# A new written-out order of work for one transformer block on one core

## The chip, the cores and the metric

The kernel runs on one core of a Trainium2 chip. The metric is the time of one execution in microseconds (us) as the device measures it; for a kernel the median of its runs is given.

## The reference

One transformer block without masks: 2048 rows of 640 numbers in bfloat16, linear attention with 32 heads of 20 features, then a gated feed-forward part with 1536 inner features. In short:

```python
x = A_x                                             # 1 x 2048 x 640
q, k, v = heads(layernorm(x) @ wqkv)                # 32 heads of 20
pq, pk  = q @ w_phi[h], k @ w_phi[h]                # per head, 20 x 20
phi_q = concat(softmax(pq), softmax(-pq))           # 40 features, phi_k likewise
kv, z = phi_k^T @ v, sum_s phi_k
o = (phi_q @ kv) / (phi_q . z + 1e-6)
h = x + o @ wo
g, u = layernorm(h) @ w_gate, layernorm(h) @ w_up
out = h + (g * u) @ w_down
```

## The kernel before, in words

The 2048 rows are 16 tiles of 128 rows (t = 0 to 15). The kernel first builds a graph of small operations, 1032 in all, each with a name, an engine, its buffers and the code that emits it. A table of text, `PLAN`, gives every operation a due time, an engine (where it may run on more than one) and the numbers of the slots that its buffers take. The function `arrange` sorts the operations by due time, and that order, engine by engine, is the program. The due times are used for nothing but the order; waits follow from the data and from who used a slot before. So a plan changes when something is issued and where it is kept, and never what is computed.

An entry reads `name:due:engine:slots`. An empty or missing engine means the operation's first choice, 1 means its second.

The names that matter here:

- `x0`, `x1`, `x3`, ... load tiles of x; `wk*`, `wv*`, `w5`, `wo*`, `wg*`, `wu*`, `wd*` load weights (line 283). Each may be issued from SP's queue (SyncE) or from that of ACT (ScalarE). `wqt*` loads a part of the Q weights transposed (line 307).
- `warm*`: matmuls on zeros that keep TensorE (PE) busy until data arrive (lines 363, 368).
- `L1s`, `L1a`, `L1l`, `L1e`, `L1n`, `xn`: mean, variance and normalisation of a tile (lines 424 to 449). `xt` transposes the normalised tile: on PE for tiles 0 and 1 (line 458), by a DMA transpose from SP's queue for the others (line 467).
- `id*`, `gl*`, `va1`, `ekz`: constants that POOL (GpSimd) writes. `gl0`, `gla`, `glb` make a block mask (lines 329 to 336).
- `Ph0`, `Ph1`, `Ph2` multiply that mask with w_phi (loaded as `w5`) into Phi (line 376). `WT` transposes the K weights on PE (line 388), `F1` and `F0` multiply Phi into the K and Q weights (line 407, the fold), `WTe`, `xte` and `Fe` copy PSUM to SBUF.
- `V`, `K`, `Q`: projections of a tile (line 478, ten matmuls of about 320 columns). `Kx`, `Ks`, `Kr`, `Ke`, `Kn` and `Qx`, `Qs`, `Qr`, `Qb`, `Qe`, `Qn`: the two softmaxes of the K and Q features over ACT, DVE (VectorE) and POOL; `Qx` is lines 547 and 549. `Ve` copies V.
- `KV`: sum of phi_k times v over all tiles (line 522). `KVe` masks it.
- `qT`: DMA transpose of phi_q from SP's queue (line 571). `N`: phi_q times KV (line 584). `dd`, `rl`, `rd`, `o` divide. `oT`: DMA transpose of o (line 615). `O`: times wo (line 621). `h` adds x. `hc`, `L2q`, `L2v`, `L2r`: second normalisation. `hT`: DMA transpose of h (line 649).
- `U<block>_<f>_<0 or 1>`: gate and up matmuls (line 664) of a block of rows; block 0 is tiles 0 and 1, block 1 tiles 2 to 5, block 2 tiles 6 to 9, block 3 tiles 10 to 13, block 4 tiles 14 and 15. `g` copies the gate, `u` multiplies (lines 669, 672). `D`: down projection of a tile (line 683), `y` scales and adds (line 695), `w` stores (line 697). Tile 15's `D` is cut into three parts.

PSUM has eight banks; V, K, Q, N, O and D take two each, a U one. Six slots hold phi_q (`ph`) and six its transpose (`phT`), so `Qx` of a tile waits until the `qT` of the tile that had the slot before has landed.

The order itself comes from these few lines:

```python
for o in sorted(G.ops, key=lambda o: (o.key, o.i)):
    o.start = o.key
    order[o.eng].append(o)
    o.alldeps = dict(o.deps)
    for b, k0 in zip(o.acq, o.slots):
        b.slots = list(range(k0, k0 + b.n))
        for k in b.slots:
            for u in last[b.pool, k].users if (b.pool, k) in last else G.init.get(b.pool, ()):
                o.alldeps.setdefault(u, u in G.init.get(b.pool, ()))
            last[b.pool, k] = b
```

Of the kernel before, what the change touches and what calls it, by code (L numbers as in the profile page):

```python
# [59 lines left out]
L1e2:12.968 L1n2:13.248 wqt2:11.56 L1n5:12.518:1 xn5:12.802::3 xt5:13.62 K1_0:12.049::6 K1_1:12.32 K1_2:12.591 K1_3:12.862 xn4:13.332::0 K1_4:13.133  # L60
Kx1_0:13.603::0 Kx1_1:14.187 V1_0:13.404::4 V1_1:13.675 K0_3:13.946 K0_4:14.217 V1_2:14.488 mk0:13.472 va1:13.532 Kx0_0:14.771::1 xt4:14.93 Kx0_1:15.355
L1s11:13.862 xn2:15.939:1:2 Ks1:14.923::0 Kr1:16.754 Ke1:17.045 L1s10:16.316 L1s7:17.103 L1a10:17.89 Kn1:17.379 wqt1:16.24 V1_3:14.759 V1_4:15.03 V0_2:15.301
V0_3:15.572 V0_4:15.843 phz:19.692 K3:16.114::6 Ve1:17.191::0 L1s6:17.999 Ve0:17.775::1 L1a11:18.786 Kx3_0:18.359::2 Kx3_1:18.943 L1a7:18.895 L1a6:19.004
L1l6:19.527 L1e6:19.853 x8:17.55 L1n6:20.408 V3:17.47::2 xt2:18.03 wqt3:19.34 K5:18.826::4 Kx5_0:20.382::3 Ks0:19.113::1 wqt4:20.65 L1n7:20.506:1 Kx5_1:20.966
V4:20.182::0 xn7:21.55:1:1 xn6:20.71::3 Kr0:22.365 L1l10:22.511 xt6:21.96 Ke0:22.693 Kn0:23.027 x12:23.27 L1e10:22.839 L1n10:25.34 Ve4:22.932::2 xt7:23.75
V5:21.538::6 Ve5:23.516::3 K2:22.894::4 V2:24.25::0 Kx2_0:24.45::4 Kx2_1:25.034 L1n11:25.564 Ks3:21.24::2 L1s8:22.633 Kr3:25.618 Ks5:23.42::3 Ve2:25.806::4
wu4:25.06 F0_4:25.606::6 Fe0_4:26.39 x14:25.54 KV0:25.925::4,5 wo0:26.02 L1a8:24.813 KV1:26.258 mk1:25.788 L1s9:24.922 L1a9:25.832 L1l8:26.974 Ve3:27.156::5
L1e8:27.74 Ks2:25.941::0 L1s13:27.334 L1a13:28.244 L1n8:28.353:1 V6:26.591::0 L1n9:28.02 Kr2:27.833 Ke2:28.124 F0_0:27.947::6 Fe0_0:28.464 Kr5:29.048 wu0:26.5
xn9:28.528::0 xt9:29.166 Kn2:28.458 xn11:29.058::2 xt11:30.476 xn8:29.588::3 xt8:31.786 Ve6:29.194::6 K4:28.266::2 L1s12:30.118 Kx4_0:29.822::1 Kx4_1:30.406
Ke3:30.99 K7:29.622::6 Ks4:31.142::1 Kx7_0:31.178::0 L1s15:32.535 L1s14:33.322 Kx7_1:31.762 xn10:34.109::1 xt10:34.747 F0_2:30.978::0 Fe0_2:32.346 Kn3:31.324  # L70
V7:31.297::2 Kr4:32.93 Ke4:33.221 rqz:33.637 wu1:36.057 Ve7:33.367::7 F0_3:32.653::6 Fe0_3:33.951 Kn4:33.674 KV2:32.972 L1a14:34.639 K6:33.305::0
# [16 lines left out]
KV11:71.629 KV12:71.962 KV13:72.295 Kn14:69.144 Ve14:71.829::7 KV14:72.628 KV15:72.961 mk2:71.457 KVe1:73.492 Q6:73.294::6 qT3:65.636::4 Qr4:72.413::0
Qb4:72.757 KVe0:73.742 N0:74.661::0 Qr13:72.951::2 dd0:75.192::0 Qe4:73.097 rd0:75.407 Qx6_0:74.859::2 qT2:69.214::5 N2:74.994::2 dd2:75.697::1 Qb13:73.295
rl2:75.913 rd2:76.267 Qn4:73.494 qT4:75.185::0 o0:75.821::0 Q7:75.327::4 oT0:76.689::0 Qx6_1:76.447 o2:76.592::1 oT2:77.999::1 Qe13:77.057 Qn13:77.364  # L90
qT13:79.309::5 N1:76.718::0 dd1:77.347::0 rd1:77.562 o1:77.976::2 Qx7_0:77.176::4 Qx7_1:77.786 N9:77.264::6 dd9:78.731::0 Q11:77.597::2 Qx11_0:79.162::5
# [833 lines left out]
```

## Time and profile before

| | us |
|---|---|
| median of 3 runs | 271.68 |
| range of the runs | 271.24 to 466.2 |
| the profiled execution | 271.81 |
| its span, first to last instruction | 270.1 |

| engine | busy us | share of the span |
|---|---|---|
| PE, matmuls | 264.2 | 98% |
| PE, weight loads (beside the matmuls) | 178.2 | 66% |
| DVE | 158.6 | 59% |
| ACT | 126.7 | 47% |
| POOL | 69.4 | 26% |

In the views of the profile, times are counted from the first instruction. In a group or a piece of the timeline, the first number is its start, the second its length, `x10` the number of instructions in it, and the square bracket the idle time of the engine ahead of it with what ended that. PEld is PE's weight load; SPq and ACTq are DMAs issued from the queues of SP and ACT. In the table by stretches, each engine has its busy time and instruction count, and PEclk is the granted clock of PE (1.00 is full). The chain is followed back from the instruction that ended last.

### The profile page before, as it was taken

To read this page: it belongs to the slowest core of one execution; us is meant where nothing else is said; L and a number is where in the kernel's file an instruction comes from. 1 tells how busy PE (TensorE), PEld (TensorE's weight loads), DVE (VectorE), ACT (ScalarE), POOL (GpSimd) and SP (SyncE) were. 2 spreads that over 40 slices of the span, in tenths; PEclk is the share of its full clock that TensorE was granted. 3 is DMA by queue.
4 is the path that set the end of the run, shared out by engine and by line. 5 is a ranking of instruction groups with operands and counts; after the bars stand their busy time and mean duration, and the time that the engine had idled before them with its cause. 6 is when DMAs were issued, how large, how long until landed. Compare 5 with 4: busy or idle time off the path is not lost.

```text
span 270.1 us, 5194 instructions
## 1 busy us (share of the span) xinstructions
PE 264.2 (98%) x2092; PEld 178.2 (66%) x2105; DVE 158.6 (59%) x299; ACT 126.7 (47%) x319; POOL 69.4 (26%) x81
## 2 busy tenths in 40 slices
PE   7999999999999999999999999999999999999996
PEld 5777777777777688756556667774554466544775
DVE  4999989887988968956855243232243131352422
ACT  3999999998677684534435021112232220122000
POOL 1365799999735301060000000000000000000000
PEclk9999999999999999999999999999999999999999
DMA  6999966699758998757820005330011000010003
GB/s 190 287 182 184 274 190 245 135 227 188 180 86 160 139 153 157 106 102 139 213 49 2 0 0 100 102 71 1 0 41 22 0 0 27 25 49 2 0 24 109
DMA packets 67944, 28.09 MB, mean 104 GB/s; under 512 B 59088, under 2 KB 66640, under 8 KB 67920
## 3 DMA queue, kind: packets, MB, share of 16 engines
q1 hardware_dynamic: 67776, 27.60, 49.0%
q8 instruction: 16, 0.26, 0.4%
q10 hardware_dynamic: 144, 0.16, 0.2%
q14 instruction: 8, 0.07, 0.1%
HBM read 11.00 MB, written 2.62 MB: 50 GB/s over the span
## 4 chain that ended last, share of the span: by engine, by line
PE 90%; DMA 4%; ACT 1%; DVE 1%; POOL 1%; issue 1%; DVEq 0%; POOLq 0%
PE ps L664 38%; PE ps L478 23%; PE ps L683 19%; PE ps L621 6%; DMA scratch<-ph 3%; PE ps L522 2%; PE ps L584 2%; PE ps L407 1%; DMA x_all<-in_A_x_dram 1%; ACT ph L547 1%; POOL Phi L376 0%; DVE st L424 0%; DVE st L425 0%; DVE Wp L695 0%; ACT gt L669 0%
## 5 line engine op out<-in xcount | busy, mean ns | idle before, releaser
L664 PE MATMUL ps<-xnT,Wgu 128*128 128x512 bf16 (+1 forms) x587 | 105.5, 335 | 0.7
L664 PEld LDWEIGHTS ps<-xnT,Wgu 128*128 128x128 bf16 x600 | 58.1, 98 | 43.4 <-DVE ev L672 0.2
L669 ACT ACTIVATE gt<-ps 128x512 bf16<-128x512 f32 (+1 forms) x60 | 29.5, 509 | 92.0 <-PE ps L664 67.9
L478 PE MATMUL ps<-Wp,xnT 128*128 128x320 bf16 (+1 forms) x480 | 68.4, 299 | 0.0
L672 DVE TENSOR_TENSOR ev<-ps,gt 128x512 bf16<-128x512 f32 (+1 forms) x60 | 33.2, 579 | 51.1 <-PE ps L664 37.0
L478 PEld LDWEIGHTS ps<-Wp,xnT 128*128 128x128 bf16 x480 | 45.5, 97 | 17.3
L683 PE MATMUL ps<-Wd,ev 128*128 128x320 bf16 (+2 forms) x396 | 53.3, 295 | 0.0
L683 PEld LDWEIGHTS ps<-Wd,ev 128*128 128x128 bf16 x396 | 38.1, 98 | 15.0 <-DVE ev L672 0.3
L514 POOL TENSOR_TENSOR ek<-ek,SR 128x1280 bf16<-128x1280 bf16 x16 | 37.6, 2361 | 5.5 <-ACT SR L499 3.2
L695 DVE SCALAR_TENSOR_TENSOR Wp<-ps,rs,x_all 128x640 bf16<-128x640 f32 (+3 forms) x18 | 14.6, 809 | 38.1 <-PE ps L683 38.0
L494 DVE TENSOR_REDUCE SR<-ek 128x64 f32<-128x1280 bf16 x16 | 23.5, 1471 | 5.1 <-ACT ek L490 4.8
L642 POOL TENSOR_SCALAR ln<-mv 128x1 f32<-128x1 f32 x4 | 0.8, 191 | 98.3 <-ACT ek L638 98.2
L552 DVE TENSOR_REDUCE S<-ph 128x66 f32<-128x1320 bf16 x16 | 24.1, 1520 | 0.2
L621 PE MATMUL ps<-Wo,Wp 128*128 128x320 bf16 x160 | 23.8, 299 | 0.0
L547 ACT ACTIVATE ph<-ps 128x600 bf16<-128x600 f32 x32 | 21.2, 677 | 4.2 <-PE ps L478 2.2
L566 POOL TENSOR_TENSOR ph<-ph,RQ 128x660 bf16<-128x660 bf16 x16 | 20.8, 1308 | 4.6 <-ACT RQ L562 4.4
L490 ACT ACTIVATE ek<-ps 128x640 bf16<-128x640 f32 x32 | 21.0, 705 | 1.9 <-PE ps L478 1.8
L621 PEld LDWEIGHTS ps<-Wo,Wp 128*128 128x128 bf16 x160 | 15.5, 98 | 6.1
L638 ACT ACTIVATE ek<-x_all,mv 128x640 bf16<-128x640 bf16 x16 | 13.1, 821 | 10.4 <-DVE x_all L627 10.3
L627 DVE SCALAR_TENSOR_TENSOR x_all<-ps,x_all 128x640 bf16<-128x640 f32 x16 | 13.1, 821 | 6.6 <-PE ps L621 6.5
L611 DVE TENSOR_TENSOR o<-ps,sm 128x660 bf16<-128x660 f32 x16 | 13.2, 836 | 0.8 <-ACT sm L604 0.6
L559 POOL TENSOR_TENSOR RQ<-RQ 128x32 f32<-128x32 f32 x15 | 3.5, 241 | 28.9 <-ACT RQ L555 28.9
(70 smaller groups left out, 169.9 us busy)
## 6 DMA issues: line engine op xcount, KB each, us to landing
out_dram<-Wp SPq DMA_DIRECT2D x15, 160.0 KB, 1.8
x_all<-in_A_x_dram SPq DMA_DIRECT2D x6, 320.0 KB, 4.5
Wgu<-in_B_w_up_dram SPq DMA_DIRECT2D x5, 384.0 KB, 6.1
Wd<-in_B_w_down_dram SPq DMA_DIRECT2D x4, 480.0 KB, 5.2
Wgu<-in_B_w_gate_dram SPq DMA_DIRECT2D x5, 384.0 KB, 4.3
ev<-in_A_wqkv_dram SPq DMA_DIRECT2D x5, 160.0 KB, 3.8
Wp<-in_A_wqkv_dram SPq DMA_DIRECT2D x5, 160.0 KB, 4.9
x_all<-in_A_x_dram SPq DMA_DIRECT2D x3, 160.0 KB, 3.1
```

The costliest lines, as they stand in the source:

```text
L478: ins = e.matmul(pb(b, hb)[:, 0:n1 - n0], lhsT=T["xnT"][:, NC - 1 - c, P * t:P * (t + 1)], rhs=T["Wp"][:, POS[kind], c, n0:n1], start=(c = ...
L490: G.op("act", "%sx%d_%d" % (nm, t, s), lambda e, s=s, b=b, ek=ek: e.activation(out=T["ek"][:, ek.slots[0], 0:2 * D].rearrange("p (b h s f) ...
L494: G.op("dve", "%ss%d" % (nm, t), lambda e, ek=ek, sr=sr: e.tensor_reduce(out=T["SR"][:, sr.slots[0], 0, :], in_=T["ek"][:, ek.slots[0], 0: ...
L514: G.op("pool", "Kn%d" % t, lambda e, eng, ek=ek, sr=sr: e.tensor_tensor(out=T["ek"][:, ek.slots[0], 0:2 * D].rearrange("p (h f) -> p h f", ...
L547: e.activation(out=v[:, 0:10].rearrange("p (b g) j f -> p b g j f", b=2), in_=pp(b, 0, 300).rearrange("p b (g j f) -> p b g j f", j=3, f=D ...
L552: G.op("dve", "Qs%d" % t, lambda e, t=t, ph=ph: e.tensor_reduce(out=T["S"][:, t, 0:66].rearrange("p (g k) -> p g k", k=6), in_=pv(ph).rear ...
L566: return e.tensor_tensor(out=v, in0=v, in1=T["RQ"][:, rq.slots[0], 1, 0:33].rearrange("p (g j) -> p g j", j=3).unsqueeze(3).to_broadcast([ ...
L621: ins = e.matmul(pb(b, hb)[:, 0:320], lhsT=T["oT"][:, oT.slots[0], c, :], rhs=T["Wo"][:, c, 320 * hb:320 * (hb + 1)], start=(c == 0), stop ...
L664: ins = e.matmul(pb(b)[:, 0:n], lhsT=T["Wgu"][:, gu, c, P * ft:P * (ft + 1)], rhs=T["xnT"][:, NC - 1 - c, o0:o0 + n], start=(c == 0), stop ...
L669: G.op("act", "g%d_%d" % (bi, ft), lambda e, pg=pg, gt=gt, n=n: e.activation(out=T["gt"][:, gt.slots[0], 0:n], in_=pb(pg)[:, 0:n], func=AF ...
L672: o_ = G.op("dve", "u%d_%d" % (bi, ft), lambda e, pu=pu, gt=gt, hh=hh, ft=ft, n=n: e.tensor_tensor(out=T["hh"][:, hh.slots[0], ft, 0:n], i ...
L683: ins = e.matmul(pb(b, hb)[:, 0:w], lhsT=T["hh"][:, hh.slots[0], ft, P * tt:P * (tt + 1)], rhs=T["Wd"][:, ft, c0 + w * hb:c0 + w * (hb + 1 ...
```

## The change

Only the table `PLAN` is replaced; graph, emitted operations and the rules of waiting are the same. Every operation is in both tables once. What differs:

- the order on all five engines and the slots of many buffers;
- the engine of 36 operations: `x1`, `wk2`, `wk3` and `w5` are issued from ACT's queue and `x3` from SP's (before, `x3` alone from ACT's); `WTe0`, `WTe1`, `xn7`, `xn14`, `Ve11`, `Ve12`, `Ve14` and `hc2` go from ACT to DVE, `WTe3`, `Ve13`, `Ve15`, `hc4`, `hc9`, `hc10`, `hc14` and `hc15` from DVE to ACT; `L1n5`, `L1n7`, `L1n8`, `L1n12`, `L1n14`, `L1n15`, `L2v3`, `L2v6`, `L2v11` and `L2v14` from DVE to POOL; `L1n10`, `Qb9`, `L2v12`, `L2v13` and `L2v15` from POOL to DVE.

The places that are spoken of below, as orders (taken from the two tables):

```
PE, start     before: ... WT1 warm20 warm21 WT0 xt0 WT3 WT2 WT4 xt1 F1_0 F1_1 F1_2 F1_3 V0_0 V0_1 K0_0 K0_1 F1_4
              after:  ... warm20 WT2 WT3 WT0 xt0 WT1 warm21 F1_2 WT4 F1_0 xt1 F1_1 F1_3 F1_4 K0_0 K0_1 K1_0
SP, start     before: x0 x1 wk1 wk2 wk0 wk3 w5 wk4 x4 wv0 wv1 x2        ACT's queue: x3
              after:  x0 x3 wk0 wk1 wk4 x4 x2 wv0 wv1                   ACT's queue: x1 wk2 wk3 w5
POOL, start   before: id0 id1 eps L1n3 gl0 gla glb Ph2 Ph0 ekz ... va1
              after:  gl0 id0 id1 eps va1 gla glb Ph2 Ph0 L1n3 ekz
DVE, start    before: L1s3 L1s0 L1a3 L1a0 L1s1 L1a1 xn0 xn3 xn1 Ph1
              after:  L1s0 L1s1 L1a0 L1a1 L1s3 L1a3 xn0 Ph1 WTe0 xn1
PE, middle    before: O9 Q12 N4 N7 Q15 O3 U0_7_0 ...
              after:  O9 Q12 N4 Q15 N7 O3 U0_10_0 U0_1_0 U0_7_0 U0_1_1 O5 U0_3_0 U0_0_0 U0_5_1 U0_0_1 N10 O4
                      U0_2_0 O7 U0_2_1 U0_5_0 N13 U0_3_1 N6 U0_4_0 U0_4_1 U0_8_0 U0_9_0 N14
SP, middle    before: qT4 oT0 oT2 qT13 oT1 oT9 qT7 oT3 hT0 hT1 oT5 qT10 oT7 oT4 qT6 hT2 qT14 hT5 hT3 oT10 hT4 oT6
              after:  qT4 oT0 oT2 oT1 qT13 oT9 qT7 oT3 hT0 hT1 oT5 qT10 oT4 oT7 qT6 hT3 hT2 hT5 qT14 oT10 hT4 qT15
PE, end       before: D14_0 D12_0 D11_0 D13_0 D10_0 D15_1 D15_2
              after:  D14_0 D12_0 D13_0 D15_0 D11_0 D10_0 D15_1 D15_2
```

The diff, cut to the lines that hold these places:

```diff
-zero:0.91 warm0:1.127 warm1:1.345 warm2:1.564 warm3:1.782 warm4:2.001 warm5:2.219 warm6:2.437 warm7:2.656 warm8:2.874::0 x3:0.78 L1s3:3.725 warm9:3.093 x0:0.78
...
-L1e1:7.441 warm20:5.926 warm21:6.036 wk2:2.22:1 wk0:2.7:1 WT0:6.546::0 WTe0:7.534 xn0:6.55::0 xt0:7.217::2 xte0:8.119 L1n3:6.138 xn3:7.08::1 wk3:3.18
-xn1:7.679::2 gl0:6.362 gla:6.524 glb:6.828 w5:3.66:1 Ph1:8.209:1 WT3:7.496::3 WT2:7.775::4 WTe2:8.703 WTe3:8.469 wk4:4.14:1 WT4:8.196::5 WTe4:8.877:1 Ph2:7.425
-xt1:8.475::6 xte1:9.285:1 Ph0:8.019 F1_0:8.754::0 Fe1_0:9.288:1 x4:4.62 wv0:5.1:1 wv1:5.58 x2:6.06 L1s4:9.693 F1_1:9.073::2 Fe1_1:9.872 ekz:8.613 F1_2:9.464::4
...
-dd5:85.766::0 rl5:86.285 h1:86.637 rd5:86.639 Qx14_1:86.819 o5:87.457::2 hT0:86.423 Qn10:87.02 O9:86.438::0 hc1:87.582::0 hT1:88.438 L2q1:88.3 Q12:87.796::6
-Qx12_0:89.361::4 N4:89.163::2 h9:88.212 Qs14:89.032 Qx12_1:89.971 oT5:89.748::1 Qr14:90.585::2 Qb14:90.929 N7:89.496::4 Qe14:91.204 Q15:89.829::0 dd4:90.467::2
-qT10:91.058::1 O3:91.196::6 dd7:90.573::3 rd7:90.788 rd4:91.078 o7:91.368::0 oT7:92.548::2 o4:92.123::1 oT4:93.858::3 L2q9:91.323 L2v9:92.878:1 U0_7_0:92.603::4
...
+zero:0.91 x0:0.78 L1s0:3.725 warm0:1.127 warm1:1.345 x1:0.78:1 L1s1:4.512 wk2:1.26 gl0:0.78 x3:1.26:1 wk3:1.74:1 warm2:1.564 wk0:1.74:1 w5:2.22 L1a0:5.299
...
+eps:1.329 L1l0:5.532 L1s3:5.531 L1a3:6.441 wk1:2.22 L1l1:5.714 L1e1:6.04 wk4:2.7:1 va1:1.359 warm13:3.966 warm14:4.185 warm15:4.403 warm16:4.621 L1e0:6.133
+xn0:6.55::0 gla:2.188 glb:2.493 Ph1:7.08:1 warm17:4.84 warm18:5.058 x4:3.18 x2:3.66 warm19:5.277 warm20:5.495 WT2:5.713::1 WTe2:6.234 WT3:6.096::2 wv0:4.14:1
+L1l3:6.819 WT0:6.546::3 WTe0:7.34:1 xt0:7.217::4 wv1:4.62 WTe3:7.001:1 L1e3:7.586 WT1:7.746::5 Ph2:6.825 wv3:5.1 wv2:5.58:1 warm21:8.025 xn1:7.748::1 Ph0:7.419
+F1_2:8.134::6 WTe1:8.278 wv4:6.06:1 xte0:7.694 L1n3:8.013 xn3:8.686::2 WT4:8.453::0 WTe4:9.216:1 x10:6.54 xt3:9.324 F1_0:8.732::1 Fe1_2:8.651:1 Fe1_0:9.249:1
...
+h1:86.437 O9:86.238::6 Q12:87.596::4 rl5:86.742 rd5:87.096 o5:87.421::2 h9:88.176 hc1:87.382::1 Qn6:86.93 N4:88.963::2 dd4:89.494::2 rd4:89.709 o4:90.123::0
+Qx14_1:88.1 hc2:90.878:1:2 Q15:89.296::0 Qx12_0:89.161::4 Qx12_1:89.771 N7:90.663::6 dd7:91.331::2 hT0:86.151 O3:91.052::4 hT1:88.238 U0_10_0:92.41::2
...
+U0_0_0:96.498::4 hc3:95.095::3 hT3:96.458 Qx15_0:95.813::3 Qx15_1:96.423 U0_5_1:97.044::5 g0_0:97.242::3 hc5:97.516::0 hT2:97.768 hT5:99.078 Qs15:97.225
...
+qT14:100.388::5 Qe15:100.081 h4:100.026 rd10:100.846 U0_2_0:99.827::0 g0_2:100.571::0 o10:101.26::2 O7:100.373::6 h7:102.015 U0_2_1:101.731::3 oT10:102.128::0
...
+U0_4_1:104.581::4 u0_4:105.925 u0_5:106.256 U0_8_0:105.127::2 U0_9_0:105.673::0 N14:106.219::6 U0_6_0:106.552::1 g0_8:106.376::3 g0_6:107.296::0
```

More of the change, by code (lines that the diff above doesn't have):

```diff
@@ L60 @@
[L60 to L71, printed above, removed]
@@ L88 @@
[L88 to L91, printed above, removed]
@@ L100 @@
-qT14:97.968::3 g0_3:98.007::3 U0_10_0:97.782::6 g0_10:98.526::2 Qs15:97.766 Qr15:99.319::3 U0_5_1:98.329::7 Qb15:99.662 Qe15:99.938 u0_1:99.201 g0_2:100.056::1
-hT5:99.458 O4:98.874::0 h4:100.431 L2q4:101.376 Qr12:102.216::0 hT3:100.768 N10:100.233::4 dd10:101.251::2 rd10:101.466 o10:101.88::2 oT10:102.749::0
-U0_3_1:100.566::2 U0_2_1:101.112::6 u0_2:102.635 U0_4_0:101.657::3 g0_4:103.087::1 hc4:102.966:1:2 hT4:104.058 O7:102.204::0 N6:103.561::4 dd6:104.093::2
-U0_4_1:103.894::6 u0_3:104.198 u0_4:104.638 U0_6_0:104.441::3 rl6:104.308 rd6:104.662 U0_5_0:104.987::2 g0_5:105.731::3 U0_6_1:105.532::6 o6:104.987::0
@@ new lines @@
+L1s8:19.049 Ks0:19.836::1 Kr0:22.021 V5:19.825::2 L1n6:21.082 xn6:21.384::2 xn7:21.914::3 Ke0:22.312 Kn0:22.646 wqt1:19.454 Ve5:22.458::3 V4:21.181::4
+Ve4:23.042::4 K2:22.537::6 Kx2_0:24.093::4 Kx2_1:24.677 L1s9:22.444 L1a9:23.354 V2:23.893::0 Ks3:23.463::2 Kr3:25.261 L1a8:24.856 Ke3:25.552 Kn3:25.886
+L1l8:25.698 L1e10:25.88 L1e8:26.024 L1n9:28.199 Ve2:26.117::5 wqt4:20.764 F0_0:25.249::2 F0_4:25.568::4 Fe0_0:26.701 smz:28.423 L1n11:28.513 K4:25.887::6
+xt6:22.074 V6:27.243::0 x12:23.384 Fe0_4:27.285 Ks5:24.965::3 Kr5:27.869 Ks2:26.358::0 Kr2:28.015 L1s13:27.751 L1a13:28.661 KV0:28.599::2,3 KV1:28.932
@@ new lines @@
+Ke2:28.306 xn9:28.77::0 xn11:29.3::1 Ve6:28.799::6 Kx4_0:29.383::1 L1s12:29.83 Kx4_1:29.967 F0_2:29.265::4 L1n8:28.737 xt7:23.864 xn8:30.617::2 K7:29.584::0
+Ke5:30.551 Fe0_2:30.697 Kx7_0:31.281::0 Kn2:28.961 wu4:25.174 V7:30.94::6 Kx7_1:31.865 Ks4:31.147::1 wd0:25.654 Ve7:32.496::7 F0_1:32.296::4 x14:26.134
+L1s14:32.54 L1s15:33.327 L1a15:34.237 L1a12:34.346 wd1:26.614 KV2:32.615 Ks7:34.455::2 Kr4:33.08 Ke4:33.371 F0_3:32.948::0 Fe0_3:33.517 KV3:33.267 Fe0_1:34.101
+K6:33.6::6 Q1_0:34.956::0 Kx6_0:35.156::4 Kx6_1:35.74 Kn5:31.274 L1a14:35.848 L1l12:36.324 Kr7:36.506 Ke7:36.797 Kn4:33.705 Q1_1:35.228 xt9:29.408 Q1_2:35.5
@@ new lines @@
+Q6:72.937::0 mk2:72.046 KVe1:73.135 KVe0:73.385 N0:74.304::4 dd0:74.835::0 rd0:75.05 Qr4:72.202::2 Qb4:72.546 Qe4:72.821 Qx6_0:74.502::5 Qx6_1:75.112
+N2:74.637::6 dd2:75.34::1 Q7:74.97::2 rl2:75.722 rd2:76.076 Qn4:73.128 qT4:74.828::0 o0:75.464::0 oT0:76.332::0 Qr13:76.256::0 Qb13:76.6 Qe13:76.875 Qn13:77.182
+N1:76.337::0 Qb10:78.447 N9:76.67::4 Qx7_0:76.994::4 Qx7_1:77.604 o2:76.401::1 dd1:77.156::0 rd1:77.371 o1:77.785::2 dd9:78.54::0 Qe10:78.722 Q11:77.298::6
+Qx11_0:78.863::2 oT2:77.642::1 Qx11_1:79.473 oT1:78.952::2 Qs7:78.646 rd9:80.081 o9:80.495::0 qT13:80.262::3 N3:78.665::2 dd3:81.25::0 Q14:78.998::0 rd3:81.465
@@ new lines @@
+O0:80.464::6 h0:82.021 Qr7:80.199::1 Qb7:80.543 Qe7:80.818 oT9:81.752::3 Qn7:81.125 qT7:83.062::2 o3:82.841::1 Qs6:83.596 Q8:81.822::4 Qx8_0:83.387::1
+Qx8_1:83.997 Qr6:85.149::2 hc0:85.295::0 O2:83.189::6 oT3:84.552::0 Qx14_0:86.013::0 h2:85.031 N5:84.547::2 dd5:85.851::0 Qb6:85.493 Qe6:86.623 O1:84.88::4
+h1:86.437 O9:86.238::6 Q12:87.596::4 rl5:86.742 rd5:87.096 o5:87.421::2 h9:88.176 hc1:87.382::1 Qn6:86.93 N4:88.963::2 dd4:89.494::2 rd4:89.709 o4:90.123::0
+Qx14_1:88.1 hc2:90.878:1:2 Q15:89.296::0 Qx12_0:89.161::4 Qx12_1:89.771 N7:90.663::6 dd7:91.331::2 hT0:86.151 O3:91.052::4 hT1:88.238 U0_10_0:92.41::2
@@ new lines @@
+rd7:91.546 o7:91.96::1 U0_1_0:92.956::3 oT5:89.548::1 Qn10:88.195 qT10:90.858::1 oT4:92.348::2 g0_1:93.7::0 g0_10:93.974::1 Qs14:92.715 Qr14:94.268::0
+Qb14:94.612 U0_7_0:93.502::6 oT7:93.658::3 h3:94.15 Qs12:94.97 qT6:94.968::4 U0_1_1:94.048::7 O5:94.594::2 h5:96.405 g0_7:94.414::2 U0_3_0:95.952::6
+U0_0_0:96.498::4 hc3:95.095::3 hT3:96.458 Qx15_0:95.813::3 Qx15_1:96.423 U0_5_1:97.044::5 g0_0:97.242::3 hc5:97.516::0 hT2:97.768 hT5:99.078 Qs15:97.225
+Qe14:98.234 U0_0_1:97.59::0 u0_0:98.66::0 u0_1:98.991 Qn14:98.541 N10:98.136::1 dd10:99.322::2 g0_3:99.111::3 O4:98.469::3 Qr15:99.385::1 Qb15:99.806
```

131 lines of the change are left out of this document (66 added, 65 removed).

## The prediction

> **What bounds the kernel now.** I read the page's head first, then the busy time by stretches, then the chain that ended last, and then the timeline of the two places where TensorE (PE) stood still.
>
> ```profile
> span 270.1 us, 5194 instructions
> PE 264.2 (98%) x2092; PEld 178.2 (66%) x2105; DVE 158.6 (59%) x299; ACT 126.7 (47%) x319; POOL 69.4 (26%) x81
> q8 instruction: 16, 0.26, 0.4%
> core 0: us, PE busy (x) PEld busy (x) DVE busy (x) ACT busy (x) POOL busy (x), PEclk, DMA share, GB/s
> 0.00:10.00 10.00, 7.87 (x70) 5.85 (x71) 6.17 (x17) 5.27 (x12) 3.13 (x14) 1.00 0.80 234
> 10.00:90.00 80.00, 80.00 (x812) 59.92 (x811) 71.78 (x114) 69.83 (x188) 57.94 (x53) 1.00 0.91 187
> 90.00:92.50 2.50, 1.95 (x25) 1.46 (x24) 2.21 (x6) 1.57 (x6) 0.24 (x1) 1.00 0.74 147
> 92.50:145.00 52.50, 52.22 (x418) 35.26 (x422) 36.38 (x80) 26.75 (x69) 7.93 (x12) 1.00 0.70 124
> 145.00:245.00 100.00, 99.58 (x611) 60.35 (x618) 34.81 (x74) 22.12 (x45) 0.19 (x1) 1.00 0.12 30
> 260.00:270.20 10.20, 7.60 (x68) 5.82 (x66) 2.95 (x5) 0.00 (x0) 0.00 (x0) 1.00 0.22 72
> ```
>
> PE is busy 264.2 of 270.1 us at the full granted clock. Its idle 5.9 us lie in four places: 2.13 in the first 10 us, 0.55 between 90 and 92.5, 2.60 behind the last matmul, and 0.28 + 0.42 as small holes between 92.5 and 245, most of which the chain books as 0.05 us of "issue" apiece at matmuls whose record is missing. The change alters no matmul, so a gain can only come out of the first two, or out of the warm-up matmuls that fill the start. That is some 3 us, about 1% of the run. It is also why a gain of over 2% (5.4 us, about what a measurement of this kernel can tell from no change) is not to be had.
>
> **The start.** The chain and the timeline:
>
> ```profile
> 0.83 3.07 DMA x_all<-in_A_x_dram
> 5.69 0.38 PE L368 MATMUL ps<-ev 128*128 128x256 bf16 x2
> 7.39 0.45 PE L458 MATMUL ps<-ident,xn 128*128 128x128 bf16 x5 [0.43 <-DVE xn L449]
> 7.13 0.26 POOL L336 TENSOR_SCALAR_AFFINE_SELECT GL<-GL 128x45 bf16<-128x45 bf16 x1
> 7.55 1.27 POOL L376 TENSOR_TENSOR Phi<-w,GL 128x280 bf16<-128x280 bf16 x2 [0.15 <-POOL GL L336]
> 7.68 1.00 PE L388 MATMUL ps<-ident,ev 128*128 128x128 bf16 x15
> 8.54 0.45 PE L458 MATMUL ps<-ident,xn 128*128 128x128 bf16 x5
> 8.40 0.60 DVE L376 TENSOR_TENSOR Phi<-w,GL 128x160 bf16<-128x160 bf16 x1
> 3.65 0.44 SPq L283 DMA_DIRECT2D w<-in_A_w_phi_dram  x1
> w<-in_A_w_phi_dram SPq DMA_DIRECT2D x1, 25.0 KB, 3.6
> 9.14 1.60 PE ps L407 x24
> 11.83 0.32 PE ps L407 x6
> ```
>
> The first real stream of PE work, the folds of line 407, starts at 9.14. It waits for Phi, whose POOL part (line 376) starts at 7.55, behind w5 (issued at 3.65, landed 3.6 later, at 7.25) and behind the GL masks, which end at 7.39; its DVE part runs from 8.40 to 9.00, behind three normalisations. The change makes the masks before w5 can arrive, puts the DVE part (Ph1) second after xn0 instead of fourth, and sends x1, wk2, wk3 and w5 from ACT's queue, so that w5 is issued at about 2.2 instead of 3.65 (it stands behind three loads, each about 0.45). With the same 3.6 it lands at 5.8, the two POOL parts take 1.27 and end at 7.1, and Ph1 ends 0.6 after xn0 (xn0 released the 7.39 matmul), at about 8.0. Then PE's own order decides: xt0 at 7.39 to 7.84, one transposed weight block at (8.54 - 7.68) / 3 = 0.29, one warm-up at 0.1 to 0.2 (two in 0.38): first fold at 8.25. At that point one weight block and one xt are still to do that were done before (0.57). So the start gains 9.14 - 8.25 - 0.57 = 0.32. Before, four folds (x24) took 1.60 where a fold alone takes 0.32, which is 0.32 of waiting, and I count a quarter of it as saved: **-0.4 us**. The best case is -0.7, all of that waiting saved. The worst is w5 landing no earlier than 7.25: POOL ends at 8.6, the first fold starts near 8.75, and 9.14 - 8.75 - 0.57 is -0.18, which the smoother folds just repay: 0. The Trainium skill speaks against me here: "DMA: Bandwidth & Descriptors", section "Issuing engines are not separate DMA queues", says that DMAs from several issuing engines run on the same 16 DMA engines and that a second issuer saves only issue time. By that rule the worst end would hold, and it stands below as a rival of its own.
>
> **The hole at 90.6.** Transposed Q features come by DMA (line 571) to N (line 584):
>
> ```profile
> 80.90 3.62 DMA scratch<-ph
> 85.26 5.29 DMA scratch<-ph
> q8 instruction: 1, 0.02, 1.0%
> 90.60 0.51 PE L584 MATMUL ps<-KVm,scratch 128*128 128x63 bf16 x11 [0.55 <-DMA scratch<-ph]
> 90.58 0.67 ACT L547 ACTIVATE ph<-ps 128x600 bf16<-128x600 f32 x1 [1.04 <-DMA scratch<-ph]
> 91.78 0.22 ACT L549 ACTIVATE ph<-ps 128x40 bf16<-128x40 f32 x1
> 91.11 1.37 PE ps L478 x10
> 92.48 1.36 PE ps L621 x10
> ```
>
> qT7, issued at 85.26, took 5.29 where qT13 before it took 3.62, and in the window 85.3 to 90.6 the DMA view shows one packet of an instruction fetch (the q8 row above is of that window); the window of qT13 shows none. The whole run has 16 such packets of 16 KB. That the fetch is the cause is my inference. N7 waited 0.55 us for qT7. The new PE order puts Q15 (1.37) ahead of N7, so N7 no longer waits: it would be ready 0.8 us after the landing. But qT7 also frees the ph slot of Qx12 on ACT, which began at 90.58 and ended its two passes at 92.00, and the new plan gives O3 the PSUM banks that Q12 held, as the old one did. So O3 cannot start before 92.05, against 92.48: the stall of 0.55 comes back as one of about 0.12, and the gain is **-0.4**. Bounds: 0 if qT7 lands 0.4 later against its neighbours, -0.55 if it lands earlier.
>
> **A wait that is added.** The rows of the SP queue behind that place:
>
> ```profile
> 91.16 1.27 SPq L615 DMA_TRANSPOSE Wp<-o  x1
> 92.49 1.45 SPq L571 DMA_TRANSPOSE scratch<-ph  x1
> 93.99 2.80 SPq L615 DMA_TRANSPOSE Wp<-o  x2
> 96.83 1.34 SPq L571 DMA_TRANSPOSE scratch<-ph  x1
> 98.22 1.60 SPq L649 DMA_TRANSPOSE xnT<-xn  x1
> 100.25 1.39 SPq L571 DMA_TRANSPOSE scratch<-ph  x1
> 97.38 2.73 PE ps L664 x25
> 110.40 0.34 PE ps L584 x11
> DMA to landing us min/median/max: 3.5/4.4/5.4
> DMA to landing us min/median/max: 4.1/4.1/4.1
> ```
>
> SP issues its transposes back to back here, one per 1.3 to 1.5 us: it is the second tightest engine. Before, qT14 was issued at 100.25, six places behind oT5, and N14 used it at 110.40, so it had 6 us to spare. The new order puts hT3 and hT5 ahead of qT14 (two more at 1.3: issue at 102.9) and moves N14 forward: between O3 and N14 stand 16 first-block matmul groups (2.73 / 5 = 0.546 each), three O (1.36) and three N (0.34), 13.8 in all. With O3 at 92.05 N14 is due at 92.05 + 1.36 + 13.8 = 107.2. qT14 lands at 102.9 + 4.1 (its own landing time before, last row) = 107.0, or at 107.3 with the median of all (4.4). So 6 us to spare become none. The row above the last bounds a landing by 3.5 and 5.4, so the wait is between 0 and 1.1. I take **+0.2**, near the end where the two middle values lie. An earlier start shifts N14 and SP alike, since SP's stretch begins with the first transposes behind N0, and so leaves the difference.
>
> **What costs nothing.** From 10 to 90 PE has no hole, and the small steps from DVE to POOL and between ACT and DVE (L1n, Ve, xn, hc, WTe) lie under it: DVE has 8 us free, ACT 10 and POOL 22 of these 80. On POOL six L1n come and one goes, while va1 moves into the idle start. If that cover fails, one late engine there costs PE a few tenths; I put +0.2 in the range. From 145 on DVE (35 of 100) and ACT (22) wait for PE, and SP is almost idle, so a new order of the U and D groups costs 0. The last three PE groups (D10, two parts of D15) are the same, and the 2.60 behind them stay.
>
> **Sum.** -0.4 - 0.4 + 0.2 = -0.6 us. The profiled execution took 271.81 us (span 270.1 and 1.7 around it), 0.13 above the median of 271.68 of the runs shown. So 271.2 against its own time, 271.1 against the median.
>
> **Rivals.**
> A. *The second queue brings nothing* (chance 0.20). For it: the nine loads ahead of the folds are many for the 234 GB/s that the first 10 us moved. Against it: the 25 KB of w5 are small and only have to be issued earlier. The start term falls to 0: 271.68 - 0.4 + 0.2 = 271.5.
> B. *Both holes close and no new one opens* (0.25). qT14 lands after 3.6 (106.5, in time) and the start gives -0.7: 271.68 - 0.7 - 0.5 = 270.5. For it: 3.6 at qT13. Against it: the SP rows just shown.
> C. *Slower: the transposes behind hT3 and hT5 come late* (0.17). If a fetch meets qT14, it lands at 102.9 + 5.4 = 108.3 and N14 waits 1.1. With the start at -0.1 and the 0.4 at 90.6 kept that is 271.68 - 0.1 - 0.4 + 1.1 = 272.3; with nothing left of the 0.4 (qT7 late once more), 272.7. It decides from a wait of 0.8 at N14 on, which is what the two gains together can pay for. To exceed 2% it would need several such places, for which I see no third row.
> D. *The fetches stay where they hurt* (0.08). The list of PE work ahead of Q12 is as long as before, so the same fetch meets qT7 again, which the 0.4 already allows for. If the gain there is 0, the time is 271.68 - 0.4 + 0.2 = 271.5. The Trainium skill ("Runtime: NRT & Kernel Launch", section "Instruction fetch mechanics") says that instructions are refilled in blocks of 16 KiB and that this is mostly hidden; the packet size agrees with the q8 row, while 5.29 against 3.62 speaks against "hidden" for a transpose in flight.
>
> **How the numbers follow.** The forecast, 271.1, has 0.30. B gives the low end, 270.2 with a little more won; C the high end, 272.7. Outside lies about 0.2, most of it above. Faster by over 2% has 0.01, slower by over 2% 0.04 (a chain of late transposes), within 2% 0.95.
>
> **What would show it.** Right: the first fold of line 407 near 8.3 instead of 9.14; no wait of line 584 for scratch near 90, with O3 a tenth or two behind Q12's exponentials; a wait of a few tenths for scratch near 106; no PE idle of note from 145 on. Wrong: a PE wait of over 0.8 us on a DMA anywhere from 20 to 120, POOL or DVE named as PE's releaser in the first stage, or a first fold after 8.8.

## The result and the profile after

The changed kernel took **274.73 us** (median of 4 runs, 273.78 to 275.38) beside 271.46 us for the kernel before: a ratio of 1.0121, 95% interval 1.0082 to 1.0161. It is slower by 3.3 us where 0.6 less was forecast, and lies above the range. Timed again later (c_after_again below), it took 273.6 beside 271.67, ratio 1.0091 (1.0055 to 1.0127). Two of the first four runs had a mean granted clock of 0.994 or 0.993, against one of six in the second; why that matters is seen below. It is not the whole difference: at full clock the first runs took 273.78 and 274.67, the second ones 273.18 to 273.94.

In the changed kernel all line numbers are one higher: the folds are L408, Phi L377, the transposed weight blocks L389. First the head of the page and the table of TensorE's (PE's) waits: for what, us in total, times, longest.

```profile
span 273.1 us, 5201 instructions
PE 266.6 (98%) x2105; PEld 179.6 (66%) x2105; DVE 160.7 (59%) x294; ACT 126.5 (46%) x319; POOL 70.9 (26%) x86
PEclk9799999999999999999999999999999999999999
PE ps L408 <- POOL Phi L377: 1.7, 1, 1.7
PE ps L364 <- DVE ev L362: 1.1, 1, 1.1
PE ps L389 <- DMA ev<-in_A_wqkv_dram: 0.6, 1, 0.6
PE ps L479 <- ACT RQ L563: 0.2, 1, 0.2
```

The same table of the kernel before:

```profile
PE ps L363 <- DVE ev L361: 1.1, 1, 1.1
PE ps L584 <- DMA scratch<-ph: 0.5, 1, 0.5
PE ps L458 <- DVE xn L449: 0.4, 1, 0.4
PE ps L388 <- DMA ev<-in_A_wqkv_dram: 0.4, 1, 0.4
PE ps L407 <- POOL ek L347: 0.2, 1, 0.2
```

The wait for the transposed features at 90 us (L584) has gone, as meant. A new wait of 1.7 us stands at the start, of the folds on POOL's Phi, and PE's busy time has grown by 2.4 us although the change alters no matmul. The digit 7 in the second slice of PEclk gives one reason: the clock was not full there. Another part lies in the records: the profile before lacks 13 of the 2105 matmuls (x2092), and some of their time counts as idle there. From the chain of the changed kernel's first 14 us, in order of time (start, length, what):

```profile
2.23 6.16 DMA w<-in_A_w_phi_dram
8.38 0.07 issue
8.45 1.41 POOL Phi L377 x2
9.87 0.09 issue
9.96 0.76 PE ps L408 x6
10.72 0.53 PE ps L389 x5
11.25 0.60 PE ps L408 x6
11.85 0.53 PE ps L459 x5
12.38 1.22 PE ps L408 x18
```

And its busy time by stretches (PE first, granted clock third from the end):

```profile
8.30:9.90 1.60, 0.00 (x0) 0.00 (x0) 1.50 (x4) 0.44 (x1) 1.45 (x3) 0.85 1.08 364
9.90:12.80 2.90, 2.84 (x29) 2.87 (x30) 1.62 (x4) 1.41 (x2) 0.44 (x2) 0.50 0.61 173
```

w5, the 25 KB that Phi is made from, was issued at 2.23 as predicted, but took **6.16 us** and landed at 8.38, later than the 7.25 of the kernel that issued it at 3.65. So the first fold starts at 9.96, 0.8 later than before, and PE stands with nothing at all to do from 8.3 to 9.9. Then it works at half clock for some 3 us: the five rows from 9.96 on take 3.64 us. At the lengths of the same pieces in c_after_again, at full clock (0.48, 0.28, 0.32, 0.28, 1.09), they would take 2.45. That is 1.2 us, on top of the standing.

### The profile page after: what moved, and what is told of

Its sections match the earlier page's. It is cut to its first block, busy times and chain, and to the rows that moved or that the text cites. A ratio compares the mean times of both kernels' runs of the same rounds, so it can differ in the third digit from the quotient of the medians.

```text
span 273.1 us, 5201 instructions
## 1 busy us (share of the span) xinstructions
PE 266.6 (98%) x2105; PEld 179.6 (66%) x2105; DVE 160.7 (59%) x294; ACT 126.5 (46%) x319; POOL 70.9 (26%) x86
## 4 chain that ended last, share of the span: by engine, by line
PE 87%; ACT 5%; DMA 4%; DVE 2%; POOL 1%; ACTq 0%; issue 0%; DVEq 0%
PE ps L665 38%; PE ps L684 19%; PE ps L479 17%; PE ps L622 8%; DMA w<-in_A_w_phi_dram 2%; ACT ph L548 2%; ACT ek L491 2%; DMA Wp<-o 2%; PE ps L408 2%; PE ps L523 1%; PE ps L585 1%; DVE RQ L560 1%; DVE SR L495 1%; DVE S L553 1%; POOL Phi L377 1%; ACT ph L550 0%
## 5 line engine op out<-in xcount | busy, mean ns | idle before, releaser
L665 PE MATMUL ps<-xnT,Wgu 128*128 128x512 bf16 (+1 forms) x600 | 107.6, 336 | 0.0
L479 PE MATMUL ps<-Wp,xnT 128*128 128x320 bf16 (+1 forms) x480 | 68.2, 299 | 0.3 <-ACT RQ L563 0.2
L479 PEld LDWEIGHTS ps<-Wp,xnT 128*128 128x128 bf16 x480 | 45.6, 97 | 18.5 <-issue 0.5
L637 ACT ACTIVATE xn<-x_all,mv 128x640 bf16<-128x640 bf16 x12 | 9.8, 820 | 3.5 <-DVE x_all L628 3.5
```

Source lines behind the costliest of these rows:

```text
L479: ins = e.matmul(pb(b, hb)[:, 0:n1 - n0], lhsT=T["xnT"][:, NC - 1 - c, P * t:P * (t + 1)], rhs=T["Wp"][:, POS[kind], c, n0:n1], start=(c = ...
L665: ins = e.matmul(pb(b)[:, 0:n], lhsT=T["Wgu"][:, gu, c, P * ft:P * (ft + 1)], rhs=T["xnT"][:, NC - 1 - c, o0:o0 + n], start=(c == 0), stop ...
```

## The experiments

Two theories: (1) the loss is the start, that is, the late w5; (2) the loss is the changed order of the middle. Every kernel is the table `PLAN` of one of the two kernels with entries altered (`name:place:engine:slots`; engine 1 is the second choice, which for w5 is SP's queue); e6, e12 and e15 change the code beside it, as shown with them.

**e1_w5_sp.** On the changed kernel:

```diff
-w5:2.22
+w5:1.7:1
```

> The changed kernel with one load moved: w5 third on SP's queue, behind x0 and x3, where the changed kernel has it fourth on ACT's queue, behind x1, wk2 and wk3. Theory 1 (the loss is the start: w5 lands at 8.38, so Phi ends at 9.87 and TensorE stands 1.70 us): w5 lands before 7, Phi is done before 8.5, the hole ahead of the first fold falls under 0.6 us, TensorE's idle time up to 20 us falls from 7.7 to about 5.5, and the kernel takes 272.0 to 272.8. Theory 2 (the loss is in the order of the middle, 20 to 110 us, and the late start is taken up by later slack): 274.3 to 274.8, start improved or not. Theory 3 (two queues at once make every load late, wherever w5 stands): w5 still lands after 8, 274 to 275.

Measured: 272.17 us, ratio 1.0019 (0.9996 to 1.0041). One load moved takes back 1.4 to 2.6 us, depending on which of the two measurements of the changed kernel it stands against (273.6 or 274.73). Pieces of its chain:

```profile
1.74 4.74 DMA ev<-in_A_wqkv_dram
8.01 0.35 PE ps L408 x6
```

The first fold starts at 8.01, and w5 is no longer in the chain (it took 4.6 us and landed at 6.3); a weight block is. Theory 1 holds for the larger part. But the first fold is now 1.1 earlier than in the kernel before, and the total is not below it.

**Start and middle apart.** e4 puts the changed start into the kernel before (all work on tiles 0, 1 and 3, loads up to x10, weight transposes, Phi, folds 0 to 3); e5 puts the old start into the changed kernel; e16 is e5 with one wait taken away that the splice itself had made.

```diff
-x3:0.78 x1:1.26 wk2:2.22:1 wk3:3.18 w5:3.66:1 ...      (e4, on the kernel before; e5 is the reverse)
+x3:1.26:1 x1:0.78:1 wk2:1.26 wk3:1.74:1 w5:2.22 ...
-Fe1_3:11.04                                            (e16, on e5)
+Fe1_3:10.9
```

> The kernel before, with the start of the changed one: order, queues, engines and buffers of all work on tiles 0, 1 and 3, the loads up to x10, the weight transposes, Phi and folds 0 to 3 from the changed kernel, everything else as before. Theory 1 (the start carries the loss): 273.8 to 274.8, with TensorE idle 7 to 8 us up to 20 us, and N7's stall of 0.7 us at 90 us still there. Theory 2 (the middle carries it): 271.0 to 271.9.

> The reverse: the changed kernel with the start of the kernel before. Theory 1 (the start carries the loss, the middle brings about +0.3): 271.2 to 272.2. Theory 2 (the middle carries it): 273.8 to 274.8.

> e5_mid_after_start_before (the changed kernel with the start of the kernel before) with the wait that the splice itself made taken away: Fe1_3 ahead of Fe1_4 on ACT (K1_3 waited 0.38 us). What is left over the kernel before is the changed order of the middle alone. If the middle costs what e5 showed less the splice: 272.1 to 272.3. If the middle costs nothing: 271.5 to 271.8.

Measured: e4 **272.46**, ratio 1.0032 (1.0010 to 1.0053), 0.85 over the kernel before; e5 **272.58**, 1.0044 (1.0015 to 1.0073), 0.97 over it; e16 272.74, 1.0052 (1.0037 to 1.0068). Neither theory's numbers came out: each half costs about 1 us. e16 lies above both of its own forecasts. In e4 w5 took 5.4 us instead of 6.2, the hole was 0.8 us, and the clock was 0.999 or 1.0 in all 12 runs. That the splice's wait went and e16 was no faster than e5 fits what e9 and e14 show further on.

**c_after_again.** The changed kernel, nothing altered.

> The changed kernel unaltered, timed again beside the kernel before: the start alone cost 0.85 us and the middle alone 0.97 us, 1.8 in sum, while the changed kernel's first four runs stood 3.3 above the kernel before. If the parts add up and those four runs were on the high side (two of them had a granted clock under 1): 273.2 to 273.8. If start and middle make each other worse: 274.3 to 275, in runs at full clock too.

Measured: 273.6, that is 1.93 over the kernel before; its five runs at full clock have a median of 273.41, 1.74 over it. 0.85 and 0.97 make 1.82, so at full clock the two halves about add up. (With e16's 1.46 for the middle they would make 2.3.) Its profiled run is one at full clock:

```profile
2.22 5.29 DMA w<-in_A_w_phi_dram
7.58 1.41 POOL Phi L377 x2
9.08 0.48 PE ps L408 x6
9.56 0.28 PE ps L389 x5
9.84 0.32 PE ps L408 x6
10.16 0.28 PE ps L459 x5
10.44 1.09 PE ps L408 x18
PE ps L389 <- DMA ev<-in_A_wqkv_dram: 1.5, 1, 1.5
PE ps L408 <- POOL Phi L377: 1.1, 1, 1.1
PE ps L585 <- DMA scratch<-ph: 0.3, 1, 0.3
```

The same w5 took 5.29 here. So its landing moves by most of a microsecond between runs, and the hole with it. The longest wait in this table, 1.5 us for a weight block, is not in the chain: a block that came earlier would have left PE standing for Phi so much longer.

**e3_loads_on_act, and the same kernel again.** One part of the change alone, on the kernel before:

```diff
-x1:1.26 wk2:2.22:1 wk3:3.18 w5:3.66:1
+x1:1.26:1 wk2:2.22 wk3:3.18:1 w5:3.66
```

> The kernel before with one part of the change alone: x1, wk2, wk3 and w5 issued on ACT's queue behind x3, at their old places in the order of issue, nothing else moved. Theory 1 (w5, with its packets of 40 bytes, lands late behind three loads of a second queue, whoever needs it): w5 lands after 7.6 where it landed at 7.26, the first fold starts later than 9.14, 271.9 to 272.8. Rival (the loads share one rate and the queue does not matter): w5 lands within 0.2 of 7.26, 271.3 to 271.8.

> e3_loads_on_act unaltered, as the control of e12 and e15 in this call, and for the granted clock: if the hole of over 2 us brings the half clock, about half of the runs or more have a granted clock of 0.994 or less and stand at 274.8 to 277, the others at 274.0 to 274.4. If four of six was chance: at most one in six below 0.998.

Measured: **274.86**, ratio 1.0140 (1.0103 to 1.0176), and 275.23, 1.0125 (1.0082 to 1.0168). Sending four loads from another queue, with no matmul moved, costs as much as the whole change, more than theory 1 had asked for. w5 took 6.89 us and landed at 9.60 (7.9 us in the second profile, at 10.6):

```profile
2.71 6.89 DMA w<-in_A_w_phi_dram
```

Of the 12 runs 8 had a granted clock of 0.994 or less; they took 274.5 to 277.7, the four others 272.9 to 274.4.

**e10_w5_back.** On e3, w5 alone back on SP's queue, where it now comes fourth:

```diff
-w5:3.66
+w5:3.66:1
```

> The kernel before with x1, wk2 and wk3 on ACT's queue and w5 on SP's, fourth, between wk0 and wk4. Against e3_loads_on_act this takes one small load back, 25 of some 500 KB. Theory 1 (what is late is w5 alone: behind the others on ACT's queue its 640 packets of 40 bytes are drained one for one with packets of 1280 bytes of SP's queue, 640 beside 665 in e3): w5 lands by 7.2, TensorE's hole ahead of the first fold is under 0.6 us, granted clock 1.0, 271.4 to 272.3. Rival (large loads on both queues are what hurts, wherever w5 stands): first fold after 9.8, 273 or more.

Measured: **271.43**, ratio 1.0006 (0.9994 to 1.0018), granted clock 0.999 or 1.0 in all 12 runs. w5 landed at 7.7, not by 7.2, but the fold waited only 0.3 us, and that for a copy on ACT. The three large loads on the second queue cost nothing. The 3.2 and 4.0 us that e3 lost against the kernel before are the place of w5 alone. On SP's queue too it took 5.5 us with the three large loads beside it on the other queue; what it won is that it landed 1.9 us before the 9.60 of e3, 2.9 before the second profile's. From e10's DMA view, and POOL's row:

```profile
w<-in_A_w_phi_dram SPq DMA_DIRECT2D x1, 25.0 KB, 5.5
7.72 1.41 POOL L376 TENSOR_TENSOR Phi<-w,GL 128x280 bf16<-128x280 bf16 x2 [0.43 <-DMA w<-in_A_w_phi_dram]
```

**Why it lands late: e15_sp_held.** On e3, SP issues x4 and all that is behind it only when w5 has landed:

```diff
-    x_b[t0:t1], key=key, before=before, also=also)
+    x_b[t0:t1], key=key, before=before, also=also,
+    after=[G.by["w5"]] if t0 == 4 else ())
```

> e3_loads_on_act with SP's queue held: x4 and all that follows it there is issued only when w5 has landed. w5 stays fifth on ACT's queue, issued at about 2.7 us. If w5 is late because its small packets take turns with SP's large ones: with none of these left w5 follows wk3 closely and lands by 8.0 (9.60 in e3), and under 300 packets of SP's queue run beside its 640 (665 in e3). If small packets on ACT's queue are slow by themselves: it lands after 9. The time of the whole kernel is no measure here, since wv0 to wv4 come some 3 us later: 273 to 277.

The DMA view of each kernel over the stretch in which w5's packets ran (queue: packets, MB, share of the 16 DMA engines; q1 is SP's queue, q10 ACT's). The changed kernel, 4.95 to 7.55:

```profile
q1 hardware_dynamic: 662, 0.77, 85.4%
q10 hardware_dynamic: 709, 0.08, 23.6%
```

The kernel before, 5.72 to 6.80, where everything is on SP's queue:

```profile
DMA packets 897, 0.30 MB, mean 281 GB/s; under 512 B 680, under 2 KB 897, under 8 KB 897
```

e3, 6.17 to 8.95, then e15, 5.72 to 7.20:

```profile
q1 hardware_dynamic: 720, 0.84, 87.7%
q10 hardware_dynamic: 724, 0.10, 24.1%
```

```profile
q10 hardware_dynamic: 743, 0.12, 48.5%
q1 hardware_dynamic: 54, 0.05, 10.0%
7.63 1.41 POOL L377 TENSOR_TENSOR Phi<-w,GL 128x280 bf16<-128x280 bf16 x2 [0.42 <-DMA w<-in_A_w_phi_dram]
```

w5 consists of 640 packets of 40 bytes (most of those "under 512 B"), 40 for each DMA engine if they are spread evenly. Where the other queue has work, its packets run beside them: 662 beside 709 and 720 beside 724 in these two profiles, 448 beside 692 in c_after_again, where the stretch lasted 1.9 us (5.05 to 6.94), and 1082 beside 708 in the second profile of e3, where it lasted 3.9 (5.97 to 9.85). One for one is thus near the middle of what was seen, not a constant. A packet of SP's queue takes 85.4% of 16 x 2.6 us / 662 = 54 ns, so 40 turns make an estimated 2.1 us for 25 KB. In the kernel before they stand in one row behind each other, and only 217 larger packets ran in that stretch, which was over in 1.1 us. Of the 2.6 us by which w5's flight grew from there to the changed kernel, the longer stretch makes 1.5; 0.65 is a longer wait for the first packet (4.95 - 2.23 against 5.72 - 3.65), and 0.4 lies between the last packet and the landing. In e15, with SP's queue all but empty, 54 ran beside them; w5, still fifth on ACT's queue, took 4.9 us instead of 6.9 to 7.9, and Phi began at 7.63 instead of 9.67. So the traffic on SP's queue makes 2.0 to 3.0 us of the flight; ACT's queue by itself does not. (e15's own time, 274.49, holds the late wv0 to wv4.)

**The clock: e6_fill and e12_fill_e3.** Warm-up matmuls in the hole ahead of the first fold, 10 in the changed kernel, 22 in e3:

```diff
-NFILL = 14
+NFILL = 24        (e6; e12: 36)
+warm22:8.126 ... warm31:8.126        (e6, ahead of F1_2; e12: warm22 to warm43 at 8.70, ahead of F1_0)
```

> The changed kernel with ten more warm-up matmuls (zeros, into a buffer that is free) on TensorE just ahead of the first fold, so that TensorE works through the 1.70 us in which it stands for Phi; Phi is as late as in the changed kernel. Theory 1a (the hole costs twice: 1.7 us of standing and then half clock for 3.4 us, which lengthened four operations by 0.25 to 0.29 us each): the first fold starts at 9.9 to 10.1 as in the changed kernel, the granted clock stays at 1.0, and the kernel takes 273.4 to 273.9. Rival 1b (the clock falls whatever stands in the hole): half clock again between 9 and 13, 274.5 to 275.

> e3_loads_on_act with 22 warm-up matmuls (zeros, into a free bank) in TensorE's hole of 2.2 us ahead of the first fold; w5 as late as there. In e3 every operation for some 3 us behind the hole took 0.26 to 0.30 us more, and 4 of 6 runs had a granted clock of 0.994 or less. If the hole brings the half clock: clock 1.0 in nearly all runs, operations behind the fold at their usual length, 272.9 to 273.6. If the fall of the clock has another cause: 274.2 to 275, clock 0.994 in half of the runs.

e6: 273.93, 1.0091 (1.0065 to 1.0118), no better than c_after_again; the clock was low in 2 of 12 runs, and in its profiled run PE had a wait of 1.2 us for a weight block ahead of the filled place. e12: 275.18, 1.0136 (1.0122 to 1.0151); one of four runs had 0.997, none less. e3 and then e12, first the hole and then 3.4 us a little behind it:

```profile
8.90:11.20 2.30, 0.03 (x1) 0.06 (x2) 1.58 (x5) 0.59 (x1) 1.53 (x3) 1.00 1.21 352
12.40:15.80 3.40, 3.40 (x22) 2.12 (x19) 2.66 (x9) 2.49 (x6) 0.26 (x1) 0.51 0.70 182
```

```profile
8.90:11.20 2.30, 2.30 (x26) 2.08 (x24) 0.76 (x3) 0.81 (x2) 0.71 (x1) 1.00 1.15 352
12.40:15.80 3.40, 3.40 (x42) 2.49 (x40) 2.66 (x10) 3.26 (x7) 0.27 (x1) 1.00 0.82 206
```

With PE at work in the hole, the 3.4 us behind it ran at full clock. They do not hold the same matmuls in both, but the eight of the first V do compare, 2.29 us in e3 and 1.25 in e12:

```profile
12.54 2.29 PE L478 MATMUL ps<-Wp,xnT 128*128 128x320 bf16 x8
13.36 1.25 PE L480 MATMUL ps<-Wp,xnT 128*128 128x320 bf16 x8
```

That agrees with the hole being what lowers the clock. But e12 was not faster than e3's median: w5 took 7.7 us in its profile, and its four runs (275.06 to 275.26) lie among e3's at low clock and above all of those at full clock. As a remedy for the time the fill failed. That the hole lowers the clock rests on the counts (low in 8 of 12 runs of e3, at most 1 of 4 of e12; 3 of 10 of the changed kernel; none of the 57 of e7, e9, e10, e13 and e14, which had no such hole), not on a gain. Against it: in 2 of 12 runs of e6, where the hole was filled, and in one of 12 of e1 and of e5, which have no hole of that size in their profiles (of other runs), the clock was low too; and in e14's profile a hole of 1.74 us at 81 us was followed by no fall. So the hole is not the only cause, and its length alone does not decide.

**The middle: e9_n7_only and e14_after_mended.** e9 swaps N7 and Q15 in the kernel before and does nothing else; e14 is e1 with two of the middle's waits taken out by order.

```diff
-N7:89.496::4 Q15:89.829::0                   (e9)
+Q15:89.496::0 N7:89.829::4
-Kx15_1:55.991 ... N14:106.219::6             (e14, on e1)
+Kx15_1:55.86 ... N14:107.1::6
```

> The kernel before with N7 and Q15 swapped and nothing else: the prediction's largest term of the middle by itself. By the prediction's sum 0.4 less than before (the 0.74 us ahead of N7 goes, about 0.3 comes back at O3): 271.0 to 271.4. Rival (later waits take it back): 271.5 to 271.8, with new idle time at O3, N14 or N15.

> e1_w5_sp with two waits of the changed kernel's middle taken away by order alone: Kx15_1 ahead of Qe9 on ACT (K13 waited 0.40 us for the bank), N14 behind U0_6_0 and U0_7_1 on TensorE (0.5 us for qT14's landing). If the middle's loss is these waits: 271.3 to 271.7. If they are passed on: 272.0 to 272.4.

e9: **271.63** beside 271.67, ratio 1.0002 (0.9994 to 1.0011). e14: 272.20, 1.0028 (1.0011 to 1.0044), against 272.17 for e1. PE's rows of e9, then two of e14 (the second from the table of waits):

```profile
91.67 0.50 PE L584 MATMUL ps<-KVm,scratch 128*128 128x63 bf16 x11
93.86 1.36 PE L664 MATMUL ps<-xnT,Wgu 128*128 128x256 bf16 x11 [0.24 <-DVE o L611]
```

```profile
83.20 1.53 PE L621 MATMUL ps<-Wo,Wp 128*128 128x320 bf16 x10 [1.74 <-DMA Wp<-o]
PE ps L522 <- DVE ev L249: 0.2, 1, 0.2
```

In e9 N7 no longer waits at 91.67, but U0_7_0, two places on, waits 0.24 us for the bank that N7 held until DVE emptied it (o7). So part of the 0.55 us was passed on; where the rest went this profile, of the slowest of e9's runs (272.0), does not show. In e14 K13 and N14 no longer wait, but KV10, next behind K13, does (0.2 us, for a result of DVE), and a late transposed o stops PE for 1.74 us in this run (273.38, 1.2 above the median).

**A version to beat both: e7_early_w5_n7 and e13_best2.** The old middle with N7 and Q15 swapped, the changed start with w5 third on SP's queue; then with its three remaining waits taken out by order.

```diff
-w5:2.22            (e7, on e4, with the swap of e9)
+w5:1.7:1
-Fe1_4:12.043:1 WTe4:9.216:1 U0_7_0:92.603::4        (e13, on e7; xn3, xt3 and g0_7 moved along)
+Fe1_4:11.6:1 WTe4:8.6:1 U0_7_0:93.72::4
```

> A kernel meant to beat both: the middle of the kernel before with N7 and Q15 swapped as in the changed kernel, and the start of the changed kernel with w5 third on SP's queue. If what was won in the first 20 us by the early w5 (TensorE idle 4.4 us there, 5.1 in the kernel before) and at N7 (0.4) is kept: 270.2 to 270.9. If later transposes, which the earlier start does not bring earlier, take it back: 271.2 to 271.9.

> e7_early_w5_n7 with its three remaining waits taken away by order alone: Fe1_4 ahead of tile 4's statistics on ACT (K1_4 waited 0.58 us for it), WTe4 ahead of xn3 on DVE (V0_0, 0.31 us), U0_7_0 two places later on TensorE (0.49 us for the bank that o7 empties). If such waits add up: 271.66 less 0.8 to 1.2, that is 270.4 to 270.9, under the kernel before. If the engine is bound elsewhere and they are passed on, as the 0.74 us of N7 were: 271.3 to 271.7.

e7: 271.66, ratio 1.0012 (0.9998 to 1.0025). e13: 272.44, 1.0036 (1.0019 to 1.0053), worse by as much as was to be won. A row of e13:

```profile
23.06 2.21 PE L478 MATMUL ps<-Wp,xnT 128*128 128x320 bf16 x15 [0.61 <-DMA xnT<-xn]
```

PE, earlier than before, now stands for a transpose of x. No version beat the kernel before; the nearest, e9, e10 and e7, are the same within their intervals.

## Why the prediction was wrong, point by point

- **The start, -0.4: wrong, and the main failure.** The step was "With the same 3.6 it lands at 5.8". The 3.6 us had been measured for w5 on SP's queue with x3 alone on the other; on ACT's queue beside the full one of SP it took 6.16 and 5.29 in the two profiles of the changed kernel. (Even on SP's queue it took 5.5 in e10, beside three loads on ACT's.) The rest of that working holds as far as the first fold: with w5 in time, e1's began at 8.01 (predicted 8.25). But e7, with that start and the old middle, is not faster than the kernel before, so the step from an earlier fold to 0.4 us of time was not borne out either. By itself the changed start costs 0.85 us at full clock (e4), and the fall of the clock adds 1.2 in the chain above.
- **Its lower bound, 0: no bound.** "The worst is w5 landing no earlier than 7.25" took over a landing from the other queue. The rule that was weighed against the forecast (the Trainium skill, "DMA: Bandwidth & Descriptors", section "Issuing engines are not separate DMA queues") speaks of a small saving, not of a loss. The rule that bears on the loss stands on the same page of the Trainium skill under "Queues, rings and completion order": each DMA engine takes turns between the queues that have work, packet by packet. The trace agrees with that, 662 packets beside 709, if what the profile counts as a packet is the page's; the prediction did not weigh it against a load of 640 tiny packets. Rival A had the right place, and priced the loss at nothing.
- **The clock: not in the prediction at all.** The Trainium skill ("TensorE: Matmul & The Clock Gate", "Part 1: The HAM clock gate") lets the clock fall to half after an idle window of about 3.4 us. Here the half clock lasted about that long, but a hole of 1.6 to 1.7 us, with 0.6 us of another ahead of it, was followed by it already; in c_after_again one of 1.1 us, with 1.5 us ahead of it, was not, and neither was e14's of 1.74. What decides between them stays open.
- **The hole at 90.6, -0.4: the trace did what was said, the time did not.** The stall at N7 went; e9, which is that step alone, moved the median by 0.04 us. The failed step is the end of the working, "a stall of about 0.12" at O3 as the only thing that comes back: the bank that N7 gives up later was the next wait, 0.24 us in e9; the rest of the 0.4 is not found. That a fetch of instructions makes such a transpose late was not tested, but the 17 profiles fit it: the 84 transposes of phi_q with a 16 KB packet of that kind in their flight have a median of 5.3 us to landing, the 188 others 3.7 (the longest 7.0).
- **The added wait at N14, +0.2 (0 to 1.1): right.** 0.3 us in c_after_again, none in the first profile of the changed kernel. (e1 has one of 0.4, and one of 0.6 at the next N.)
- **"What costs nothing", 10 to 90 us: wrong.** All that is changed behind the start costs about 1 us with the old start (e5 0.97, e16 1.46), and some 0.6 with the mended one (e1, whose interval still holds 1, and e14). One new wait is in the profile of every kernel with the changed middle but e14's, where it was mended: L479 on ACT (0.2 us, at 59 us). Others move from run to run: 0.93 us for L479 at 31 us in e16, 1.74 us for a transpose in e14. That DVE, ACT and POOL had idle time on average said nothing of when each result is due. But waits are not seen to make up the loss: from 20 to 180 us PE stands 0.67 us in e5 and 0.93 in the kernel before (some of it at matmuls whose record is missing). Which entry of the middle carries the loss, and by what, is open.
- **From 145 on, 0: right.** PE is busy all 90.00 us of the stretch from 180 to 270 in the changed kernel; no new wait stands there.
- **What was named as a sign of error came:** a first fold after 8.8 (9.96), and POOL as PE's releaser in the first stage.
- **What a measurement can tell: too coarse.** The prediction put it at about 2%; the intervals here are 0.2 to 0.8% wide.

The rows for the stretch from 145 on (the changed kernel, 180 to 270) and for the wait in e16:

```profile
180.00:270.00 90.00, 90.00 (x534) 51.80 (x532) 28.45 (x52) 15.01 (x29) 0.00 (x0) 1.00 0.06 20
31.57 2.62 PE L479 MATMUL ps<-Wp,xnT 128*128 128x320 bf16 x18 [0.93 <-ACT ek L491]
```

## What to carry to other kernels

Before a load is moved to a second queue, count its packets, not its bytes: here the small load of tiny packets, for which much waited, landed earlier in the queue of the large ones (e10), and earliest ahead of the traffic (e1). A landing time belongs to the queue and the neighbours with which it was measured. And where an engine is busy 98% of the time, a stall taken away by order is often passed to the next bank or transpose: e9, e13, e14 and e16 each removed what the profile named and won nothing.
